# Key weights in three loads, x in four copies, and a new order for all work, in an attention and GLU kernel

## Chip, cores and metric

One NeuronCore of one Trainium2 chip runs the whole kernel. The metric is device time in microseconds (us), lower is better. Shorter names for the engines: PE is TensorE (matmuls; PEld its weight loads), DVE is VectorE, ACT is ScalarE, POOL is GpSimd, SP is SyncE, which here only issues DMAs.

## What is computed

x has 2048 tokens of 512 values in bf16. The output is a gated mix of two branches:

```python
g = sigmoid((x * gate_w).sum(-1))
a = A(x, wq, wk, wv, wo, beta)     # 32 heads of 16, 4 segments of 512 tokens
b = B(x, w_gate, w_up, w_down)     # (gelu(x @ w_gate) * (x @ w_up)) @ w_down, 1792 wide
out = g * a + (1 - g) * b
```

In A, each segment has causal softmax attention within itself (`a_dot`), and reads a memory that earlier segments wrote: `a_mem = phi(q) M / phi(q) z`, where `phi(t)` is `t + 1` above zero and `exp(t)` below, `M` sums `phi(k)` times v, and `z` sums `phi(k)`. The two are mixed by `sigmoid(beta)` of the head, and the result is multiplied by `wo`.

## The kernel before

The work is cut into some thousand tasks: a task is one or several instructions of one engine, with what it reads and writes (L68, class Task). The order of all tasks is a list written into the file, `ORDER`; `schedule` (L129) walks it, takes the PSUM bank that stands behind the colon for a task that opens one (`K0_1a:1`), or the engine for an eviction that may run on two (`Kev0_0:d` is DVE, `:a` is ACT). Each engine then runs its own tasks in the order of the list, and `finalize` (L189) puts a semaphore wait in front of an instruction for what other engines or DMAs must have done first. So a task that waits holds up everything behind it on its engine, and SP's queue of DMA issues is one such engine. The place of a load in the list does not say when it is issued: SP issues each as soon as its own waits and those ahead of it are over.

Names of tasks, with segment s and tile t of four:

- `ld_...`: loads (`ld_w`, L340 to 341). x of segment 0 comes in two ways: tokens 0 to 255 as two plain loads of 128 KB (`ld_x0_0` on SP, `ld_x0_1` on ACT), and tokens 256 to 511 by two transposing DMAs (`ld_x0_t2`, `ld_x0_t3`, L361). The key weights come as two loads of 256 KB, blocks 2 and 3 on SP (`ld_wk1`), blocks 0 and 1 on ACT (`ld_wk0`).
- `warm1`, `warm2` (L383): matmuls on constants that only keep PE busy. `xtr0_p` (L786): PE transposes of the first 256 tokens into PSUM; `xev0_p` (L795): copies of them to SBUF.
- `K0_ta`, `K0_tb`, `K0_tc` (L477): key projections of segment 0, in blocks 2 and 3 on the first 256 tokens, blocks 0 and 1 on them, and all blocks on tokens 256 to 511. `Ks_t`, `Qs_t`, `Gs_ft`, `Us_ft` (L449): other projections, 4 matmuls of 512 columns each. `Vs_ma`, `Vs_mb` (L499): value projections. `Kev`, `Qev`, `Gev`, `Vev` (L442 to 443, L506 to 507): evictions from PSUM.
- `kpada`, `kpadb` (L488): masked copies of the keys that the score matmuls load as weights.
- `sts_tA` to `E` (L602): fills of PSUM with scores; there is one PSUM area for them. `exps_...` (L609): the exponential of a fill on ACT, 2048 wide; the next fill waits for it. `msks_...` (L615): causal masks on POOL. `pvs_t` (L644): reads of the values, 128 small matmuls for two tiles, which take half of the values from `vsh`, a copy with the partitions' halves swapped.
- `vshs_mj` (L518): DMAs on SP that make `vsh`. `ktrs_t` (L573): DMA transposes of phi(k); `otrs_c` (L564): of the memory's output.
- `pha`, `phb`, `phc` (L461 to 465): phi on DVE, ACT, DVE. `mz` (L577), `nd` (L547): memory write and read on PE.
- `gelu`, `gd` (L698, L703): gelu on ACT; `h` (L720): the product with the up projection; `out` (L735), `wo` (L749): last products; `wev`, `oev` (L740 to 753): their evictions; `dma` (L757): stores.
- `ld_beta`, `betab` (L764): the heads' gates, loaded and copied. `ld_gw`, `gwz`, `gwtr`, `gwev` (L354, L769, L771): the gate vector, made into a 513th column of the value weights.

Of the kernel before, what the change touches and what calls it, by code (L numbers as in the profile page):

```python
# [248 lines left out]
def _build(es, nc, A_x, A_wq, A_wk, A_wv, A_wo, A_beta, B_w_gate, B_w_up, B_w_down, gate_w, out):  # L249
# [132 lines left out]
    for name, n, cols in (("warm1", 45, 80), ("warm2", 7, 80)):  # L382
        one(name, PE, 3.0, [I(lambda e, cols=cols: e.matmul(BK[s0.i][:, 0:cols], ones, ones[:, 0:cols], start=True, stop=True),  # L383
                              [], [bk(s0)]) for _ in range(n)], bias=9000.0, opens=name == "warm1")
# [400 lines left out]
    for p in (1, 0):  # L785
        one(f"xtr0_{p}", PE, 4 * T_TR, [I(lambda e, q=q, kb=kb, p=p: e.transpose(  # L786
            XB[:, 1024 * p + (kb % 2) * 256 + q * 128:1024 * p + (kb % 2) * 256 + q * 128 + 128],
            pt[stage[0]][:, q, kb * 128:(kb + 1) * 128], ident[:, :]),
            [("xs", 0, 0), ("xs", 0, 1), ("pt", stage[0]), ("ident",)], [("X", p)]) for kb in (2 * p, 2 * p + 1) for q in (0, 1)])
        dst = xT[0][:, 2 * p:2 * p + 2, 0:256]  # L790
        xin = XB[:, 1024 * p:1024 * p + 512].rearrange("p (k c) -> p k c", c=256)
        wr = [("xT", 0, kb, "h0") for kb in (2 * p, 2 * p + 1)]
        task(f"xev0_{p}", [
            (ACT, 0.477, [I(lambda e, dst=dst, xin=xin: e.activation(dst, xin, ACTF.Copy), [("X", p)], wr)]),
            (DVE, 0.335, [I(lambda e, dst=dst, xin=xin: e.tensor_copy(dst, xin), [("X", p)], wr)])], L_DVE)  # L795
# [67 lines left out]
ld_x0_0 ld_wk1 ld_x0_1 warm1:0 ident xtr0_1 xev0_1:d xtr0_0 warm2 xev0_0:d vones0 masks ld_wk0 causal1 gwz ld_x0_t2 ld_x0_t3 ld_wq0 ld_wq1 ld_gw  # L863
causal0 consts K0_1a:1 K0_3a:2 K0_3b K0_2a:3 K0_0a:0 K0_2b K0_0b K0_1b K0_0c K0_2c K0_3c K0_1c Kev0_0:d Kev0_2:d kpadb0_0 kpadb0_2 causal kpada0_0
Kev0_3:a Q0_0:0 ld_wg0b Qev0_0:a Q0_1:3 st0_0A gwtr:2 Kev0_1:d gwev Q0_3:0 ld_wv ld_wg0 Qev0_1:d V0_1b:1 V0_3a:2 V0_3b:3 exp0_0A Qev0_3:d Vev0_3a:a
Vev0_1b:a st0_0B Vev0_3b:d kpada0_2 kpada0_1 V0_0b:0 V0_1a:2 V0_2a:1 Vev0_0b:d G0_6:3 Gev0_6:d Vev0_1a:d Vev0_2a:d exp0_0B st0_0C exp0_0C Q0_2:0
G0_2:3 V0_2b:2 ld_x1_2 ld_x1_1 ld_x1_3 ld_x1_0 ld_beta st0_0D Vev0_2b:a exp0_0D Gev0_2:d kpadb0_1 Qev0_2:d phka0_0 V1_2b:1 V0_0a:3 G1_6:2 V1_0b:0
Vev1_2b:d phka0_2 st0_0E Vev0_0a:d Vev1_0b:d G0_1:1 Gev1_6:a exp0_0E Gev0_1:d Q1_2:3 V1_3b:2 V1_3a:0 kpada0_3 Qev1_2:d Vev1_3a:d phkb0_2 phkc0_2
Vev1_3b:d st0_1A gz0 exp0_1A gr0 Q1_0:1 V1_0a:3 G1_5:0 Vev1_0a:d Gev1_5:d st0_1B Q1_1:2 K1_0:3 exp0_1B phkb0_0 ld_wu1 ld_x2_0 G0_5:0 Qev1_0:d kpadb0_3
vsh0_21 st0_1C exp0_1C Qev1_1:d ld_x2_1 ld_x2_3 ktr0_3 ld_wg1 Gev0_5:d V1_2a:1 K1_3:2 K1_1:0 vsh0_01 Vev1_2a:a vsh0_20 ld_x2_2 ktr0_2 vsh0_00 ld_wd1  # L870
st0_1D phkc0_0 betab Kev1_1:d kpada1_1 G0_4:1 G0_3:0 Gev0_4:d Kev1_0:d Gev0_3:d Kev1_3:a ld_wd0 ld_wu0 ktr0_1 ktr0_0 vsh1_20 ld_wo V1_1a:2 Vev1_1a:d
exp0_1D bexp st0_2A exp0_2A msk0_0B msk0_0D msk0_0C kpada1_0 msk0_0E goa0 gob0 msk0_0A msk0_1A msk0_1C msk0_1D gqa gfull msk0_1B G0_0:1 Q1_3:3 G1_1:0
Qev1_3:d phqa1_0 st0_2B Gev0_0:d gqb Gev1_1:a pv0_1:2301 exp0_2B tp0_d01 tp0_d00 pvp0_01 Q2_0:3 Qev2_0:d tp0_d11 st0_2C K1_2:2 Kev1_2:d pvp0_00
tp0_d10 gelu0 G0_8:3 G0_13:1 gd0_13 G0_10:2 G0_11:0 G0_9:1 gd0_8 gd0_10 gd0_9 gd0_11 G0_12:3 G0_7:2 gd0_12 G1_2:1 U0_0:0 gd0_7 Gev1_2:d pvp0_11 h0_0
U0_13:3 U0_10:2 h0_10 Q2_1:1 Qev2_1:d exp0_2C st0_2D mz0:0 U0_7:2 U0_9:1 pvp0_10 h0_13 exp0_2D phqb1_0 st0_2E exp0_2E phka1_0 h0_7 mza0 h0_9 ota0_0
phqa1_2 kpadb1_0 G1_4:3 U0_1:2 h0_1 Gev1_4:a V1_1b:0 st0_3A G1_0:1 U0_5:3 Q2_2:2 exp0_3A Vev1_1b:a Gev1_0:a Qev2_2:a kpadb1_1 st0_3B exp0_3B U0_11:0
U0_4:1 U0_12:2 st0_3C phkb1_0 exp0_3C phqc1_0 kpada1_2 h0_4 h0_5 U0_6:1 U0_2:3 h0_11 h0_12 phqb1_2 h0_2 G1_3:0 Gev1_3:d h0_6 kpadb1_2 st0_3D phka1_2
U0_3:2 h0_3 U0_8:3 h0_8 Q2_3:0 Qev2_3:d exp0_3D phkb1_2 msk0_2A msk0_2B msk0_2C msk0_3A msk0_2E msk0_2D msk0_3C goc0 msk0_3B st1_0A msk0_3D pv0_3:1230
exp1_0A st1_0B exp1_0B tp0_d20 tp0_d21 pvp0_20 tp0_d30 ota0_1 pvp0_21 tp0_d31 kpada1_3 out0_1_0:1 out0_1_1 out0_1_2 V2_0a:2 Vev2_0a:d G1_9:3 V2_1b:0
Vev2_1b:d wev0_1:d st1_0C G1_8:2 G1_10:0 G1_11:1 gelu1 gd1_9 G1_7:3 gd1_8 gd1_10 gd1_7 gd1_11 G1_13:2 gd1_13 G1_12:0 gd1_12 phqc1_2 phkc1_0 mzq0  # L880
pvp0_31 pvp0_30 ota0_3 V2_0b:3 Vev2_0b:d ota0_2 V2_1a:1 Vev2_1a:d out0_0_0:2 out0_0_1 out0_0_2 nd1_0:0 ndp1_0 phkc1_2 exp1_0C st1_0D exp1_0D K2_0:3
K2_2:1 wev0_0:d Kev2_0:d Kev2_2:a K2_1:0 st1_0E Kev2_1:d U1_2:2 h1_2 wo0_1:1 nd1_3:3 nd1_1:0 exp1_0E st1_1A ld_x3_2 vsh1_00 vsh2_01 ktr1_1 ktr1_0
oev0_1 ndp1_1 wo0_0:2 oev0_0 kpada2_0 vsh1_21 out0_2_0:1 nd1_2:0 msk1_0C msk1_0A exp1_1A st1_1B exp1_1B msk1_0B gz1 msk1_0E msk1_1A msk1_0D msk1_1B
out0_2_1 wo0_2:2 ndp1_2 st1_1C exp1_1C nd1_5:0 out0_2_2 ndp1_3 wev0_2:a ndp1_5 out0_3_0:3 st1_1D nd1_4:0 out0_3_1 out0_3_2 ktr1_2 dma0 vsh1_01 otr1_3
ndp1_4 otr1_0 oev0_2 phka2_0 msk1_1C wev0_3:d ktr1_3 dma1 vsh2_00 otr1_1 ld_x3_1 ld_x3_0 ld_x3_3 exp1_1D st1_2A exp1_2A gr1 msk1_1D pv1_1:1023 st1_2B
exp1_2B tp1_d01 tp1_d00 kpadb1_3 V2_2b:0 Vev2_2b:d K2_3:1 Kev2_3:a G2_3:0 pvp1_00 Gev2_3:d tp1_d10 st1_2C U1_8:1 G2_1:0 otr1_2 V2_3a:2 h1_8 Gev2_1:d
Vev2_3a:d kpadb2_0 kpadb2_1 exp1_2C st1_2D phkb2_0 exp1_2D G2_6:1 wo0_3:0 U1_3:2 pvp1_01 tp1_d11 Gev2_6:a h1_3 phka2_2 oev0_3 st1_2E U1_0:3 V2_3b:1
G2_0:2 Gev2_0:d h1_0 Vev2_3b:d exp1_2E phkb2_2 st1_3A mz1:0 G2_4:2 G2_5:3 pvp1_10 mza1 Gev2_5:d exp1_3A st1_3B exp1_3B Gev2_4:d U1_11:1 G2_2:0
Gev2_2:d ota1_0 U1_13:3 h1_13 U1_10:2 h1_10 h1_11 G2_11:0 G2_10:3 pvp1_11 phkc2_0 phkc2_2 ota1_1 otm1_0 otm1_1 G2_12:2 G2_9:1 st1_3C gelu2 gd2_11
gd2_12 G2_7:0 G2_13:2 gd2_10 gd2_9 gd2_7 gd2_13 G2_8:3 gd2_8 U1_7:1 U2_9:0 K3_0:2 h1_7 U2_5:3 Q3_0:1 phqa2_0 h2_9 h2_5 Qev3_0:d Kev3_0:d exp1_3C  # L890
st1_3D exp1_3D U1_1:0 U2_12:3 msk1_3A msk1_2A msk1_3B U2_13:1 h2_12 h1_1 h2_13 kpada2_1 st2_0A U1_9:2 V2_2a:3 U2_7:0 msk1_2D msk1_2B msk1_2E h1_9
Vev2_2a:d vsh2_20 dma2 dma3 ktr2_0 ktr2_2 vsh2_21 exp2_0A phqb2_0 msk1_3D msk1_2C msk1_3C st2_0B h2_7 kpada2_2 pv1_3:1230 tp1_d21 exp2_0B tp1_d20
V3_1a:2 Vev3_1a:a st2_0C exp2_0C pvp1_21 tp1_d31 U1_6:1 Q3_1:2 V3_0a:0 st2_0D h1_6 pvp1_20 Vev3_0a:d Qev3_1:a V3_2b:1 U1_4:2 U1_5:0 exp2_0D st2_0E
exp2_0E tp1_d30 phqc2_0 h1_5 h1_4 ota1_2 Vev3_2b:a U1_12:3 h1_12 pvp1_31 pvp1_30 out1_1_0:0 st2_1A V3_1b:2 out1_1_1 V3_3a:3 exp2_1A st2_1B msk2_0B
msk2_0D Vev3_3a:a exp2_1B out1_1_2 U2_4:1 msk2_0E goa1 gob1 kpadb2_3 kpada2_3 msk2_0C msk2_0A msk2_1A ota1_3 h2_4 otm1_2 otm1_3 K3_1:3 mzq1 Vev3_1b:a
wev1_1:a st2_1C msk2_1B goc1 U2_1:2 Q3_3:1 V3_0b:0 Kev3_1:d kpada3_0 h2_1 Qev3_3:d kpadb2_2 exp2_1C msk2_1C st2_1D V3_2a:3 U2_6:2 exp2_1D Vev3_2a:a
wo1_1:1 Vev3_0b:d kpadb3_0 h2_6 oev1_1 st2_2A msk2_1D pv2_1:0231 exp2_2A st2_2B exp2_2B tp2_d00 pvp2_00 phqa2_2 tp2_d01 tp2_d10 pvp2_10 pvp2_01
tp2_d11 out1_0_0:0 out1_0_1 st2_2C phqb2_2 out1_0_2 V3_3b:2 Vev3_3b:d wev1_0:d out1_3_0:3 phqc2_2 pvp2_11 exp2_2C st2_2D exp2_2D wo1_0:1 out1_3_1
# [46 lines left out]
```

## Time and profile before

| | us |
|---|---|
| median of 3 runs | 263.83 (263.21 to 263.96) |
| the profiled execution | 264.41 |
| its span, first to last instruction | 262.7 |
| PE busy in it | 254.5 |
| ACT busy | 203.2 |
| DVE busy | 198.1 |

The profile is of one execution. Its rows give start and duration in us from the span's start, line, engine, operation, tiles written and read, and in brackets the idle time of the engine before and what ended it. A row of a group gives busy time, the mean duration in ns, and the idle time just ahead of the group's instructions.

### The profile page before, as it was taken

What the parts mean: (1) busy time and instruction counts of PE and PEld (TensorE: products, weight loads), DVE (VectorE), ACT (ScalarE), POOL (GpSimd) and SP (SyncE); (2) the same over time, 40 slices, a digit from 0 to 9 for tenths busy, and PEclk for the clock granted to TensorE, in tenths of its full rate; (3) what the DMA queues carried; (4) which work ended last, traced back from release to release, by engine and by line L of the source; (5) the groups of instructions that cost most, each with busy time, mean ns of one, the idle gap of its engine ahead of it and who ended that gap; (6) DMA issues with size and microseconds to landing.
All of it is one profiled execution on the core that took longest, in us unless ns stands there. A gap on an engine that the chain in (4) does not pass through costs nothing.

```text
span 262.7 us, 6672 instructions
## 1 busy us (share of the span) xinstructions
PE 254.5 (97%) x2815; PEld 122.6 (47%) x2849; DVE 198.1 (75%) x412; ACT 203.2 (77%) x171; POOL 98.3 (37%) x163
## 2 busy tenths in 40 slices
PE   7999999999999999999999999999999999999995
...
DMA packets 31990, 16.50 MB, mean 63 GB/s; under 512 B 21592, under 2 KB 31960, under 8 KB 31960
## 3 DMA queue, kind: packets, MB, share of 16 engines
...
q10 hardware_dynamic: 688, 0.85, 0.9%
...
## 4 chain that ended last, share of the span: by engine, by line
PE 88%; DVE 6%; ACT 3%; issue 2%; DVEq 0%
PE psD L449 41%; PE psD L735 19%; PE psX L602 8%; PE psD L644 6%; PE psD L749 5%; PE psD L499 5%; PE psD L547 1%; ACT gb L698 1%; PE psD L383 1%; PE psD L477 1%; DVE kT L443 1%; DVE gb L443 1%; ACT pt L609 1%; PE psD L577 1%; DVE phk L461 1%
## 5 line engine op out<-in xcount | busy, mean ns | idle before, releaser
L609 ACT ACTIVATE pt<-psX 128x2048 bf16<-128x2048 f32 x72 | 135.1, 1877 | 28.3 <-PE psX L602 26.7
L615 POOL TENSOR_TENSOR pt<-pt,ctri 128x256 bf16<-128x256 bf16 x128 | 91.7, 727 | 129.4 <-ACT pt L609 124.9
L449 PE MATMUL psD<-xT,wu 128*128 128x512 bf16 x214 | 52.7, 380 | 1.3 <-issue 1.1
L449 PE MATMUL psD<-xT,wg 128*128 128x512 bf16 x216 | 52.3, 379 | 0.8 <-issue 0.3
L735 PE MATMUL psD<-wd,gb 128*128 128x512 bf16 x217 | 51.8, 379 | 0.8 <-issue 0.5
L720 DVE TENSOR_TENSOR gb<-psD,gb 128x512 bf16<-128x512 f32 x56 | 37.2, 681 | 10.8 <-PE psD L449 10.8
L449 PEld LDWEIGHTS psD<-xT,wg 128*128 128x128 bf16 x224 | 20.7, 98 | 24.7 <-issue 1.3
L735 PEld LDWEIGHTS psD<-wd,gb 128*128 128x128 bf16 x224 | 20.7, 98 | 24.3 <-issue 2.1
L449 PEld LDWEIGHTS psD<-xT,wu 128*128 128x128 bf16 x224 | 20.2, 98 | 24.8 <-issue 2.6
L602 PE MATMUL psX<-qT,kD 32*128 32x192 bf16 (+7 forms) x512 | 28.5, 287 | 0.0
L530 DVE STREAM_TRANSPOSE tT<-psD 128x512 f32<-128x512 f32 x32 | 21.7, 701 | 5.5 <-PE psD L644 5.0
L443 DVE CAST gb<-psD 128x512 bf16<-128x512 f32 x20 | 13.6, 687 | 12.8 <-PE psD L449 12.8
L602 PEld LDWEIGHTS psX<-qT,kD 32*128 32x128 bf16 x512 | 8.2, 92 | 25.1 <-ACT pt L609 13.6
L499 PE MATMUL psD<-wv,xT 128*128 128x257 bf16 (+1 forms) x128 | 18.2, 273 | 0.0
L753 DVE SCALAR_TENSOR_TENSOR ost<-psD,gtok,wds 128x512 bf16<-128x512 f32 (+1 forms) x17 | 11.9, 710 | 7.9 <-PE psD L749 7.8
L668 DVE SCALAR_TENSOR_TENSOR ob<-tT,gq,rc 128x256 bf16<-128x256 f32 x32 | 16.7, 522 | 1.1
L703 ACT ACTIVATE gb<-psD 128x512 bf16<-128x512 f32 x28 | 15.0, 595 | 3.3 <-PE psD L449 3.3
L644 PE MATMUL psD<-pt,vsh 64*17 64x192 bf16 (+7 forms) x512 | 17.1, 283 | 0.0
L644 PE MATMUL psD<-pt,vnat 64*17 64x192 bf16 (+7 forms) x512 | 17.1, 283 | 0.0
L449 PE MATMUL psD<-xT,wq 128*128 128x512 bf16 x60 | 15.6, 379 | 0.4 <-issue 0.2
L749 PE MATMUL psD<-wo,oT 128*128 128x512 bf16 (+1 forms) x66 | 15.7, 367 | 0.2 <-issue 0.2
L499 PEld LDWEIGHTS psD<-wv,xT 128*128 128x128 bf16 x128 | 11.8, 97 | 6.6 <-issue 1.3
...
## 6 DMA issues: line engine op xcount, KB each, us to landing
...
vsh<-vnat SPq DMA_DIRECT2D x16, 68.0 KB, 2.7
...
wq<-in_A_wq_dram SPq DMA_DIRECT2D x2, 256.0 KB, 3.7
...
```

The costliest lines, as they stand in the source:

```text
L443: (DVE, 0.60, [I(lambda e: e.tensor_copy(dst, src()), [bk(sl), *reads], writes)]),
L449: one(name, PE, n * T_MM, [I(lambda e, i=i: e.matmul(BK[sl.i][:, :], lhs(i), rhs(i), start=(i == 0), stop=(i == n - 1)), reads(i), [bk(sl) ...
L499: one(f"V{s}_{m}{'ab'[hf]}", PE, 2 * T_MM, [I(lambda e, i=i, sl=sl, a=a, z=z, xs=xs: e.matmul(BK[sl.i][:, 0:z - a], xs(i), wv[:, i, a:z], ...
L530: one(f"tp{name}", DVE, 0.605, [I(lambda e, sl=sl, ti=ti: e.transpose(tT[ti][:, :], BK[sl.i][:, :]), [bk(sl)], [("tT", ti)])], bias=bias)
L602: ins.append(I(lambda e, t=t, kb=kb, ncol=ncol, c0=c0, g=g: e.matmul(XALL[:, g * 512 + c0:g * 512 + c0 + ncol], kD[(4 * s + t) % R_KD][32 ...
L609: one(f"exp{s}_{name}", ACT, 2048 * 0.000833 + 0.05, [I(lambda e: e.activation(pt[slot][:, :, :], xin, ACTF.Exp, scale=ATT_SCALE), [("X",) ...
L615: ins.append(I(lambda e, mv=mv: e.tensor_tensor(mv, mv, cm, ALU.mult), [("pt", slot), ("causal",)], [("pt", slot)]))
L644: ins.append(I(lambda e, kb=kb, slot=slot, c0=c0, n=n, g=g, r0=r0, sl=banks[j], va=va: e.matmul(BK[sl.i][32 * g:32 * g + 17, 64 * kb:512], ...
L668: I(lambda e, ti=ti, ri=ri, t=t, j=j, dst=dst: e.scalar_tensor_tensor(out=dst, in0=t_rows(ti), scalar=gq[:, 2 * t + j:2 * t + j + 1], in1= ...
L720: one(f"h{s}_{ft}", DVE, 0.605, [I(lambda e, sl=sl, gi=gi, f=f: e.tensor_tensor(gb[gi][:, f, :], BK[sl.i][:, :], gb[gi][:, f, :], ALU.mult ...
L735: mm.append(I(lambda e, fb=fb, gi=gi, f=f, q=q, sl=sl: e.matmul(BK[sl.i][:, :], gb[gi][:, f, q], wd[:, fb, :], start=(fb == 0), stop=(fb = ...
L749: one(f"wo{s}_{qt}{sfx}", PE, 4 * T_MM * w / 512, [I(lambda e, kb=kb, q=q, so=so, c=c, w=w: e.matmul(BK[so.i][:, 0:w], oT[:, kb, q], wo[:, ...
```

## The change

The loads of the key weights are three, in the queues of SP, ACT and ACT; the transposes and copies of x go by block, four of each on smaller tiles; the warming matmuls are one run of 52 with 66 columns:

```diff
-    for eng, h in ((SP, 1), (ACT, 0)):
-        ld_w(f"wk{h}", eng, wk[:, halves[h], :], wsrc(A_wk)[:, halves[h], :], [("wk", 2 * h), ("wk", 2 * h + 1)], 0.25)
+    for eng, nm, c in ((SP, "2", slice(2, 3)), (ACT, "3", slice(3, 4)), (ACT, "0", slice(0, 2))):
+        ld_w(f"wk{nm}", eng, wk[:, c, :], wsrc(A_wk)[:, c, :], [("wk", i) for i in range(c.start, c.stop)], 0.125)
...
-    for name, n, cols in (("warm1", 45, 80), ("warm2", 7, 80)):
+    one("warm1", PE, 3.0, [I(lambda e: e.matmul(BK[s0.i][:, 0:66], ones, ones[:, 0:66], start=True, stop=True),
+                             [], [bk(s0)]) for _ in range(52)], bias=9000.0, opens=True)
...
-    for p in (1, 0):
-        one(f"xtr0_{p}", PE, 4 * T_TR, [...
+    for kb in (2, 3, 0, 1):
+        one(f"xtr0_{kb}", PE, 2 * T_TR, [...
...
-            (DVE, 0.335, [I(lambda e, dst=dst, xin=xin: e.tensor_copy(dst, xin), [("X", p)], wr)])], L_DVE)
+            (DVE, 0.25, [I(lambda e, dst=dst, xin=xin: e.tensor_copy(dst, xin), [("X", kb)], wr)])], L_DVE)
```

The list `ORDER` is another one throughout. Its beginning before:

```
ld_x0_0 ld_wk1 ld_x0_1 warm1:0 ident xtr0_1 xev0_1:d xtr0_0 warm2 xev0_0:d vones0 masks ld_wk0 causal1 gwz ld_x0_t2 ld_x0_t3 ld_wq0 ld_wq1 ld_gw
causal0 consts K0_1a:1 K0_3a:2 K0_3b K0_2a:3 K0_0a:0 K0_2b K0_0b K0_1b K0_0c K0_2c K0_3c K0_1c Kev0_0:d Kev0_2:d kpadb0_0 kpadb0_2 causal kpada0_0
Kev0_3:a Q0_0:0 ...
```

and after:

```
ld_x0_1 ld_wk3 ld_wk0 warm1:0 ld_x0_0 causal1 ident xtr0_2 xtr0_3 xtr0_0 xtr0_1 vones0 ld_wk2 ld_x0_t2 ld_x0_t3 ld_wq0 gwz xev0_3:d masks xev0_1:a
xev0_0:a xev0_2:d K0_1a:1 K0_3a:2 K0_0a:3 K0_3b K0_1b K0_2a:0 K0_1c Kev0_1:d K0_3c Kev0_3:a kpadb0_1 kpadb0_3 K0_0b K0_0c K0_2b Kev0_0:a phka0_0
kpada0_0 ld_wq1 ld_gw ld_wg0b ld_wv ld_wg0 Q0_0:1 Q0_2:2 ... st0_0A exp0_0A K0_2c ...
... Gev0_2:d Qev0_2:d G0_5:1 V1_2b:3 G1_6:2 betab kpada0_1 Gev1_6:d st0_0E ...
... exp0_1C K1_3:2 Vev1_2a:a phkc0_2 st0_1D Kev1_1:d kpada1_1 G0_3:0 G0_4:1 vsh1_20 vsh0_20 vsh0_00 ld_wd1 ktr0_2 exp0_1D Gev0_4:a kpadb0_2 st0_2A exp0_2A ... Q1_3:3 V1_1a:0 Vev1_1a:a G0_0:1 st0_2B ... pv0_1:3021 ...
```

SP's queue from the second segment's x on was, before: `vsh0_21`, x of segment 2, `ktr0_3`, `ld_wg1`, `vsh0_01`, `vsh0_20`, x, `ktr0_2`, `vsh0_00`, `ld_wd1`, `ld_wd0`, `ld_wu0`, `ktr0_1`, `ktr0_0`, `vsh1_20`, `ld_wo`. After, it is: `ktr0_0`, `vsh0_21`, x, `vsh0_01`, `ld_wg1`, x, `vsh1_20`, `vsh0_20`, `vsh0_00`, `ld_wd1`, `ktr0_2`, `ktr0_3`, `ld_wd0`, `ld_wu0`, `ktr0_1`, and so on, with `ld_wo` behind the second segment's transposes.

More of the change, by code (lines that the diff above doesn't have):

```diff
@@ L381, in _build @@
     ones = nc.const_aps.tensor(1.0, [P, P], BF)
-    for name, n, cols in (("warm1", 45, 80), ("warm2", 7, 80)):
-        one(name, PE, 3.0, [I(lambda e, cols=cols: e.matmul(BK[s0.i][:, 0:cols], ones, ones[:, 0:cols], start=True, stop=True),
-                              [], [bk(s0)]) for _ in range(n)], bias=9000.0, opens=name == "warm1")
+    one("warm1", PE, 3.0, [I(lambda e: e.matmul(BK[s0.i][:, 0:66], ones, ones[:, 0:66], start=True, stop=True),
+                             [], [bk(s0)]) for _ in range(52)], bias=9000.0, opens=True)
     cn = [
@@ L784, in _build @@
     XB = XALL.bitcast(BF)
-    for p in (1, 0):
-        one(f"xtr0_{p}", PE, 4 * T_TR, [I(lambda e, q=q, kb=kb, p=p: e.transpose(
-            XB[:, 1024 * p + (kb % 2) * 256 + q * 128:1024 * p + (kb % 2) * 256 + q * 128 + 128],
+    for kb in (2, 3, 0, 1):
+        one(f"xtr0_{kb}", PE, 2 * T_TR, [I(lambda e, q=q, kb=kb: e.transpose(
+            XB[:, 1024 * kb + q * 128:1024 * kb + q * 128 + 128],
             pt[stage[0]][:, q, kb * 128:(kb + 1) * 128], ident[:, :]),
[L789 to L795, printed above, removed]
+            [("xs", 0, 0), ("xs", 0, 1), ("pt", stage[0]), ("ident",)], [("X", kb)]) for q in (0, 1)])
+        dst, xin, wr = xT[0][:, kb, 0:256], XB[:, 1024 * kb:1024 * kb + 256], [("xT", 0, kb, "h0")]
+        task(f"xev0_{kb}", [
+            (ACT, 0.38, [I(lambda e, dst=dst, xin=xin: e.activation(dst, xin, ACTF.Copy), [("X", kb)], wr)]),
+            (DVE, 0.25, [I(lambda e, dst=dst, xin=xin: e.tensor_copy(dst, xin), [("X", kb)], wr)])], L_DVE)
     head_gates()
@@ L862 @@
 ORDER = """
[L863 to L898, printed above, removed]
@@ L899 @@
-st2_2E nd2_0:2 out1_2_0:0 out1_3_2 msk2_2C gz2 gr2 gz3 gr3 goa3 ndp2_0 gob3 oev1_0 msk2_2D goc3 goa2 gob2 exp2_2E st2_3A exp2_3A msk2_3A msk2_2B
-wev1_3:d G3_4:2 nd2_2:1 out1_2_1 Gev3_4:a ndp2_2 st2_3B exp2_3B nd2_4:3 G3_1:1 Gev3_1:d out1_2_2 nd2_1:2 st2_3C dma4 ktr2_1 vsh3_20 vsh3_01 ktr2_3
-dma5 ndp2_4 ndp2_1 G3_3:1 wo1_3:3 exp2_3C Gev3_3:a K3_2:2 st2_3D wev1_2:a msk2_2A kpada3_1 oev1_3 Kev3_2:d nd2_5:1 nd2_3:3 G3_0:0 G3_5:2 ndp2_3 ndp2_5
-Gev3_0:d msk2_3C msk2_2E exp2_3D st3_0A exp3_0A goc2 msk2_3D msk2_3B G3_2:3 wo1_2:1 Gev3_2:d G3_6:0 Gev3_6:a Gev3_5:d oev1_2 ota2_0 st3_0B pv2_3:3210
```

14 lines of the change are left out of this document (1 added, 13 removed).

## The prediction

> **What bounds the kernel now.** I read the page's shares and slices first, then who waited for whom on PE, then the chain that ended last, then the first 12 us in order of time.
>
> ```profile
> span 262.7 us, 6672 instructions
> PE 254.5 (97%) x2815; PEld 122.6 (47%) x2849; DVE 198.1 (75%) x412; ACT 203.2 (77%) x171; POOL 98.3 (37%) x163
> ...
> PE   7999999999999999999999999999999999999995
> ...
> PE 88%; DVE 6%; ACT 3%; issue 2%; DVEq 0%
> ...
> L449 PE MATMUL psD<-xT,wu 128*128 128x512 bf16 x214 | 52.7, 380 | 1.3 <-issue 1.1
> ```
>
> The second row gives PE 254.5 of 262.7 us; the slices show it full from the second to the last but one. A busy PE need not be a fast one, since matmuls overlap, so I look for idle time and for the pace:
>
> ```profile
> PE psD L477 <- DVE omem L354: 0.6, 1, 0.6
> PE psD L449 <- issue: 1.8, 11, 0.2
> ```
>
> ```profile
> 0.82 3.16 PE psD L383 x45
> ...
> 5.30 0.38 issue
> 5.91 2.71 PE psD L477 x20
> ...
> 9.97 1.67 PE psD L449 x7
> ...
> 12.97 1.32 PE psD L499 x12
> ...
> 16.90 0.33 PE psX L602 x8
> 17.23 1.85 PE psD L449 x8
> ...
> 42.86 8.31 PE psD L449 x38
> ...
> 258.00 0.82 PE psD L749 x3
> 258.91 0.60 issue
> ```
>
> The only wait of PE above 0.2 us is the 0.6 before the first key projection (L477; the release is put down to a memset, but the chain shows plain waiting from 5.30). After it, 38 matmuls of 512 columns take 8.31 us, 0.216 each, at the end of the span as in the middle. So **PE is the bound from 5.9 us to the tail**. The change adds no PE work behind the head: the same projections, fills, reads and outputs stand in both orders. A new order can therefore gain only in the head, or lose by making PE wait. The forecast is a sum of differences on the profiled 264.41 us; that run is 0.58 above the median of 263.83 (263.21 to 263.96), and I put the same difference on the median.
>
> **The head.** Rows in order of time, and the landing times of the DMAs:
>
> ```profile
> 1.22 0.46 ACTq L341 DMA_DIRECT2D wk<-in_A_wk_dram  x1
> 1.25 0.41 SPq L341 DMA_DIRECT2D wk<-in_A_wk_dram  x1
> ...
> 3.78 1.05 PE L786 MATMUL psX<-ident,pt 128*128 128x128 bf16 x8
> ...
> 4.44 0.85 DVE L795 COPY xT<-psX 128x512 bf16<-128x512 bf16 x2 [4.44 <-PE psX L786]
> ...
> 5.91 4.01 PE L477 MATMUL psD<-xT,wk 128*128 128x256 bf16 x32 [0.61 <-DVE omem L354]
> ...
> 6.77 0.39 SPq L341 DMA_DIRECT2D wv<-in_A_wv_dram  x1
> ```
>
> ```profile
> wk<-in_A_wk_dram ACTq DMA_DIRECT2D x1, 256.0 KB, 5.0
> wk<-in_A_wk_dram SPq DMA_DIRECT2D x1, 256.0 KB, 4.5
> ```
>
> ```profile
> L361 SPq DMA_TRANSPOSE xT<-in_A_x_dram x2: 1261/1272/1282, 1.7 to 3.0; - x2
> ...
> DMA to landing us min/median/max: 4.2/4.6/5.0
> ```
>
> SP's half of the key weights (blocks 2 and 3, the ones used first) lands at 1.25 + 4.5 = 5.75, and the first projection starts at 5.91. x is copied by 4.44 + 0.85 = 5.29, so the weights were last, by about 0.5 us.
>
> In the changed kernel blocks 2 and 3 come as 128 KB each, SP and ACT, second in their queues; blocks 0 and 1 are ACT's third. Half the bytes stand before the first projection. x is copied in four parts, xev0_3 and xev0_2 on DVE, 1 and 0 on ACT. The transposes to PSUM are the same eight. xev0_3 can start at 4.44 as before; two copies of half the size cost at least the 0.42 of one big one and, with a fixed share, about 0.58, so the first projection can start at 5.0 to 5.1: **at most 0.83 sooner** (5.91 - 5.08). The split gives x itself nothing.
>
> How much of that lives? The third group of key matmuls (columns 256 on) needs both DMA transposes of x; the second is issued at 1.71 + 1.28 + the queue, 3.04, and lands 4.2 later, at 7.24 (the other at 1.7 + 5.0 = 6.7, which is when wv, waiting for it, is issued: 6.77). Before, 16 small matmuls stand in front of that group; in the new order 12 do (K0_1a 3a 0a, K0_3b 1b, K0_2a). Twelve at 0.11 (12 in 1.32) are 1.3 us, a little more while the pace is slow, so from 5.1 they end at about 6.6 to 7.0, and K0_1c waits until 7.3. From there 20 of 32 are left: the last would start at 7.3 + 19 x 0.11 = 9.39, against 9.92 - 0.27 = 9.65 before. **Head: -0.26.** Bounds: -0.83 (all of it kept) and +0.45 (the pieces land like ACT's half, 1.22 + 5.0 = 6.22, and twelve matmuls follow). The query weights follow SP's transposes in both; gate vector: gwz is moved ahead of the copies on DVE, so its load no longer waits for that memset, but wv behind it still waits for the 6.7 landing. Worth nothing, and its use, gwtr, stands far behind. The 52 warming matmuls of 66 columns in one run instead of 45 and 7 of 80 end before x lands: nothing, unless the pace changes (rival 3).
>
> **A later limit on the lead.** In the new order DVE runs betab ahead of kpada0_1, which the fill st0_0E needs; before, betab came at 32 us.
>
> ```profile
> 16.08 0.58 SPq L341 DMA_DIRECT2D omem<-in_A_beta_dram  x1
> ```
>
> ```profile
> omem<-in_A_beta_dram SPq DMA_DIRECT2D x1, 8.0 KB, 4.9
> ```
>
> ```profile
> 19.71 0.34 DVE L488 TENSOR_SCALAR kD<-kT,maskB 128x512 bf16<-128x512 bf16 x1
> ...
> 22.05 0.40 PE L602 MATMUL psX<-qT,kD 32*128 32x256 bf16 x8
> ...
> 32.56 1.25 DVE L764 COPY betab<-omem 32x8 bf16<-32x8 bf16 x4
> ```
>
> Beta lands at 16.08 + 4.9 = 20.98 in either order, since SP's queue before it is paced by wv. With 1.25 for the four copies (0.7 if nothing slows the last) and 0.34 for kpada, st0_0E's second half can go at 22.0 to 22.6. The row at 22.05 is st0_0E before; in the new order G0_5 (0.86 by the pace) stands ahead of it in place of V1_0b (0.44), so with the lead of 0.26 PE is there at 22.2, and at the second half 0.15 later. I take 0.1, bounds 0 to 0.3. Any further lead would be lost here.
>
> **One fill too early.** A fill, its exponential and the next fill form a loop:
>
> ```profile
> 213.50 0.40 PE L602 MATMUL psX<-qT,kD 32*128 32x448 bf16 x8
> ...
> 213.96 1.88 ACT L609 ACTIVATE pt<-psX 128x2048 bf16<-128x2048 f32 x1 [0.42 <-PE psX L602]
> ...
> 215.89 0.40 PE L602 MATMUL psX<-qT,kD 32*128 32x384 bf16 x8
> ```
>
> That is 2.39 from fill to fill. Wherever the PE work between two fills is shorter, PE waits. The old order has at least eight big and three small matmuls between any two. The new one has st0_1D, G0_3, G0_4, st0_2A: 0.33 + 1.85 = 2.18 (the rows at 16.90 and 17.23). **+0.2**, and nothing else can fill it, since PE is in order. Bounds 0 to 0.3.
>
> **The rest.** I compared, fill by fill, the PE work with ACT's work between exponentials. From st0_2B the two orders have nearly the same intervals; at two places ACT has an eviction or a phi exponential more than before (st2_0A, st2_1D). Each overruns by under 0.1. I take +0.1, bounds -0.3 (small waits that the old order has and the new has not) to +0.5. The tail has the same last five groups on PE and the same evictions: 0.
>
> Sum: -0.26 + 0.1 + 0.2 + 0.1 = +0.14, so **264.0 us**. This case's own range is 263.2 to 264.7.
>
> **Rivals.**
>
> 1. *The lead is kept.* SP's queue holds 128 KB less ahead of the transposes; if they land half a microsecond sooner, 0.83 can stay: 263.83 - 0.83 = 263.0. For it: wk alone was late. Against it: the same bytes move in all, and beta. 262.6 to 263.4.
>
> 2. *The shifted V copies become the wait (slower).* In SP's queue vsh1_20 now stands ahead of vsh0_20 and vsh0_00, which the first value read pv0_1 needs. vsh1_20 waits for Vev1_2a, an ACT eviction right behind exp0_1C (0.38). Two issues of 0.61 follow, so vsh0_00 is issued 1.6 us after exp0_1C ends. PE reaches pv0_1 after st0_1D to st0_2A (2.39), st0_2A to st0_2B (0.33 + 2.26), and st0_2B (0.33): 5.4 us after it. That leaves 3.8 for the landing.
>
> ```profile
> 32.93 0.38 ACT L507 ACTIVATE vnat<-psD 128x256 bf16<-128x256 f32 x1
> ```
>
> ```profile
> vsh<-vnat SPq DMA_DIRECT2D x3, 68.0 KB, 4.6
> ```
>
> ```profile
> L518 SPq DMA_DIRECT2D vsh<-vnat x16: 597/611/1514, 24.5 to 194.0; - x16
> ...
> DMA to landing us min/median/max: 2.0/2.7/6.1
> ```
>
> The first of these is from 30 to 35.2 us, behind a 896 KB load, as here. It decides at 3.8: at 4.6 PE loses 0.8 (264.8), at 6.1 2.3 (266.3). For it: the loads of this stage. Against it: one transpose fewer in front, and 2.7 over all. I give it 264.9.
>
> 3. *The slow pace lasts longer.* 45 matmuls of 80 columns take 3.16 us, 0.070 each, while 256 columns later take 0.11: PE starts at half pace although the granted clock shows full in every slice. The key matmuls still begin slow: 31 x 0.11 and one of 0.27 are 3.7, they take 4.01, so some three ran at half pace. The new head has 728 columns less of warming (52 x 66 against 52 x 80), none of it between the transposes and the first projection. [...] From rows: with all 32 key matmuls at half pace they take 32 x 0.11 = 3.5 more, less the 0.3 paid already. I take half of that, 264.0 + 1.6 = 265.6, between 264.4 and 267.2.
>
> 4. *The pieces are not reported sooner.* ACT's half, issued first, landed 0.5 us after SP's. If wk3 on ACT waits for the transposes, K0_1a stands at 6.2: the +0.45 above instead of -0.26, 264.7 at most, 264.5 with what the slow pace no longer costs. [...]
>
> **How the numbers follow.** Forecast 0.37, rival 1 0.20, rival 2 0.21, rival 3 0.12, rival 4 0.10. About 0.3% (0.8 us) is what a measurement of this kernel can tell from no change: under 263.04 is faster, over 264.62 slower. Faster: 0.14 of rival 1 and 0.03 of the forecast, 0.17. Slower: 0.18 of rival 2, 0.12 of rival 3, 0.03 of rival 4, 0.04 of the forecast, 0.37. Within: 0.46. The range, with a tenth left out at each end: 262.9 to 265.7.
>
> **What would show it.** The first L477 matmul at 5.0 to 5.2 and a gap of PE before the matmuls of the third group; a wait of a fill for DVE (kD) near 22 us; a wait of L602 for ACT near 35 us of 0.2; no PE gap at the first L644. Wrong if L477 starts at 5.9 or later, if its 32 matmuls take over 5 us without a gap (rival 3), if L644 waits for a DMA (rival 2), or if PE idles somewhere after 60 us, where I saw no cause.

## The result, and the profile after

The changed kernel took **266.03 us** (median of 6 runs, 264.96 to 266.90), the kernel before 263.75 (6 runs, 263.00 to 263.96): ratio 1.0084, 95% interval 1.0065 to 1.0104. The forecast was 264.0, with a range up to 265.7. (The same kernel in another set of six runs, a_again below, has a median of 265.31.) The runs of the changed kernel lie twice as far apart as those before. Its profiled execution took 265.86, span 264.1: 1.45 us over the profiled 264.41.

From the page of the changed kernel (its lines from 383 on stand one lower than before, L643 for L644):

```profile
span 264.1 us, 6703 instructions
...
PE   8999999999999999999999999999999999899995
...
q8 instruction: 22, 0.36, 0.6%
...
PE 89%; DMA 5%; SPq 2%; issue 1%; DVE 1%; ACT 1%; DVEq 0%
```

TensorE is as full as before, but for a dent near the end, and a DMA has come into the chain. Who waited for whom on TensorE in the changed kernel:

```profile
PE psD L643 <- issue: 0.9, 1, 0.9
PE psD L382 <- PEq L875: 0.8, 1, 0.8
PE psX L601 <- DVE kD L487: 0.4, 1, 0.4
PE psD L476 <- DVE xT L792: 0.4, 1, 0.4
PE psX L601 <- ACT pt L608: 0.2, 1, 0.2
```

L382 is the warming, L476 the first keys. Three lines are new: a fill (L601) waits 0.4 for VectorE's kD, a fill waits 0.2 for ScalarE, and a value matmul (L643) stands 0.9 us for "issue", which means for nothing that the profile shows. The places, in order of time on TensorE:

```profile
4.96 3.79 PE L476 MATMUL psD<-xT,wk 128*128 128x256 bf16 x28 [0.36 <-DVE xT L792]
```

```profile
22.44 0.29 PE L601 MATMUL psX<-qT,kD 32*128 32x256 bf16 x4 [0.41 <-DVE kD L487]
```

```profile
226.03 0.31 PE L643 MATMUL psD<-pt,vnat 64*17 64x320 bf16 x4
227.25 0.26 PE L643 MATMUL psD<-pt,vsh 64*17 64x192 bf16 x4 [0.91 <-issue]
```

The first is the head: keys begin at 4.96, 0.95 before the old 5.91. The second is the second half of st0_0E behind beta. The third stands in the middle of pv3_1, the 128 value matmuls at 224 us: 112 are done, and the next ones start 1.2 us later.

To compare the two orders I use TensorE's **lag**: the start of a group less the work of all matmuls from the first key on (from the first key to the last group of four 251.9 us in both orders). "Behind pv3_1" is the next fill, st3_2C. b_before and a_again are second profiles of the kernel before and of the changed kernel; a_store6 and a_beta are edits of the latter, shown further down.

```
                first key   st0_0E  st0_1A  st0_2A  pv3_1  behind pv3_1   last
before            5.88       6.28    6.29    6.41    7.00      6.99       7.11
b_before          5.66       5.83    5.84    5.96    6.52      6.51       6.63
after             4.96       5.54    6.14    6.47    7.17      8.48       8.59
a_again           4.85       5.64    6.55    6.88    7.59      7.79       7.90
a_store6          4.73       5.25    6.11    6.44    7.17      8.79       8.91
a_beta            4.73       5.17    5.18    5.50    6.20      6.39       6.51
```

After less before, in the two profiles first shown: head -0.74, beta's fill +0.59 (0.60 against 0.01), st0_1A to st0_2A +0.21, from there to pv3_1 +0.11, pv3_1 +1.32, the rest -0.01. Sum +1.48, against 1.45 of the clock. The table says more. The pause in pv3_1 is in some executions only; a_again, without it, has +0.20 in that column, so that 1.1 of the 1.32 is the pause. Beta costs 0.60 to 0.91, and the old head of b_before is 0.45 better than that of the first profile.

### The profile page after: what moved, and what is told of

It is laid out like the page before. It is cut to its first block, busy times and chain, and to the rows that moved or that the text cites. A ratio compares the mean times of both kernels' runs of the same rounds, so it can differ in the third digit from the quotient of the medians.

```text
span 264.1 us, 6703 instructions
## 1 busy us (share of the span) xinstructions
PE 258.1 (98%) x2849; PEld 121.8 (46%) x2849; DVE 195.7 (74%) x403; ACT 207.5 (79%) x182; POOL 96.9 (37%) x163
## 4 chain that ended last, share of the span: by engine, by line
PE 89%; DMA 5%; SPq 2%; issue 1%; DVE 1%; ACT 1%; DVEq 0%
PE psD L448 44%; PE psD L734 19%; PE psX L601 9%; PE psD L643 6%; PE psD L748 5%; PE psD L498 4%; SPq L345 2%; DMA omem<-in_A_beta_dram 2%; DMA xT<-in_A_x_dram 2%; DMA wv<-in_A_wv_dram 2%; PE psD L546 1%; ACT pt L608 1%; PE psD L576 1%; DVE ost L752 0%; SPq L341 0%
## 5 line engine op out<-in xcount | busy, mean ns | idle before, releaser
L614 POOL TENSOR_TENSOR pt<-pt,ctri 128x256 bf16<-128x256 bf16 x128 | 89.2, 708 | 128.1 <-ACT pt L608 105.2
L448 PE MATMUL psD<-xT,wu 128*128 128x512 bf16 x224 | 54.7, 380 | 0.0
L719 DVE TENSOR_TENSOR gb<-psD,gb 128x512 bf16<-128x512 f32 x56 | 37.9, 685 | 21.5 <-PE psD L448 21.0
L734 PE MATMUL psD<-wd,gb 128*128 128x512 bf16 x224 | 53.5, 380 | 0.0
L448 PE MATMUL psD<-xT,wg 128*128 128x512 bf16 x224 | 53.0, 379 | 0.0
L601 PE MATMUL psX<-qT,kD 32*128 32x192 bf16 (+7 forms) x512 | 28.7, 287 | 0.7 <-DVE kD L487 0.4
L601 PEld LDWEIGHTS psX<-qT,kD 32*128 32x128 bf16 x512 | 8.4, 92 | 26.0 <-ACT pt L608 10.9
L643 PE MATMUL psD<-pt,vsh 64*17 64x192 bf16 (+7 forms) x512 | 17.4, 283 | 0.9 <-issue 0.9
L702 ACT ACTIVATE gb<-psD 128x512 bf16<-128x512 f32 x28 | 15.6, 593 | 3.1 <-PE psD L448 2.8
L498 PE MATMUL psD<-wv,xT 128*128 128x256 bf16 (+1 forms) x128 | 17.9, 273 | 0.0
L643 PE MATMUL psD<-pt,vnat 64*17 64x192 bf16 (+7 forms) x512 | 17.4, 283 | 0.0
L739 ACT ACTIVATE wds<-psD,omgt 128x512 f32<-128x512 f32 x7 | 4.7, 685 | 12.6 <-PE psD L734 12.6
```

What stands on the lines that cost most here:

```text
L448: one(name, PE, n * T_MM, [I(lambda e, i=i: e.matmul(BK[sl.i][:, :], lhs(i), rhs(i), start=(i == 0), stop=(i == n - 1)), reads(i), [bk(sl) ...
L498: one(f"V{s}_{m}{'ab'[hf]}", PE, 2 * T_MM, [I(lambda e, i=i, sl=sl, a=a, z=z, xs=xs: e.matmul(BK[sl.i][:, 0:z - a], xs(i), wv[:, i, a:z], ...
L601: ins.append(I(lambda e, t=t, kb=kb, ncol=ncol, c0=c0, g=g: e.matmul(XALL[:, g * 512 + c0:g * 512 + c0 + ncol], kD[(4 * s + t) % R_KD][32 ...
L614: ins.append(I(lambda e, mv=mv: e.tensor_tensor(mv, mv, cm, ALU.mult), [("pt", slot), ("causal",)], [("pt", slot)]))
L643: ins.append(I(lambda e, kb=kb, slot=slot, c0=c0, n=n, g=g, r0=r0, sl=banks[j], va=va: e.matmul(BK[sl.i][32 * g:32 * g + 17, 64 * kb:512], ...
L702: t = one(f"gd{s}_{ft}", ACT, 0.485, [I(lambda e, gi=gi, f=f, sl=sl: e.activation(gb[gi][:, f, :], BK[sl.i][:, :], ACTF.Gelu_apprx_tanh), ...
```

## The experiments

The runs a_, b_, c_, d_ and e_ are five sets, each on a chip of its own, beside runs of the kernel before on the same chip; that one's medians lay between 263.56 and 263.64.

### a_again, a_split4, a_store6, a_beta: which of the losses counts

a_again is the changed kernel unedited.

> The changed kernel once more, nothing edited. In its first profile TensorE stood still for 1.2 us (226.04 to 227.25) in the middle of the 128 value matmuls pv3_1, waiting for nothing that the profile names, and a 16 KB packet of the instruction queue q8 had begun at 224.54 and taken 1.32 us. Theory F (the instruction block that holds the rest of pv3_1 comes too late): the pause is at the same matmul again, 0.5 to 2 us long, and the time is 265 to 267. Theory B (the loss sits in the head, where st0_0E waits for beta, and the pause was an accident of one execution): no pause in pv3_1, the time is still 265.5 to 266.5, and the wait before the second half of st0_0E is 1 us or more.

265.31 (264.23 to 265.72, 6 runs), ratio 1.0064 (1.0042 to 1.0086). Its profile has no pause in pv3_1, and a longer wait for beta; each theory has a part right: the time is in F's range, and the pause is missing as B said, but the wait before the second half of st0_0E is 0.7 where B said 1 or more. TensorE's waits in a_again:

```profile
PE psX L601 <- DVE kD L487: 0.7, 1, 0.7
PE psD L476 <- DMA wk<-in_A_wk_dram: 0.3, 1, 0.3
```

a_split4:

```
+ cuts = (slice(0, 256), slice(256, 512)) if name in ("U2_10", "U2_2", "U3_13", "U2_11") else (slice(0, 512),)
- one(name, ..., [I(lambda e, i=i: e.matmul(BK[sl.i][:, :], lhs(i), rhs(i), ...)) for i in range(n)], ...)
+ one(name, ..., [I(lambda e, i=i, c=c: e.matmul(BK[sl.i][:, c], lhs(i), rhs(i)[:, c], ...)) for c in cuts for i in range(n)], ...)
```

> The changed kernel with four of its up projections between pv2_3 and pv3_1 (U2_10, U2_2, U3_13, U2_11) written as two half-wide matmuls for each full one: the same work, but 32 more TensorE instructions ahead of pv3_1, so that every border between instruction blocks lies 32 instructions earlier in the program from there on. Theory F: the fetch is then asked for well before pv3_1, the pause in pv3_1 is gone, and the time is 264.3 to 264.9 (266.0 less the 1.3 that the pause cost, or a little more). Theory B: the borders do not matter, the time is 266.0 or up to 0.1 more. Should the fetch be asked for no earlier, the pause only moves 16 matmuls ahead within pv3_1.

264.70 (264.21 to 266.46, 11 runs): the median as by theory F and no pause in its profile, but five runs at 265.4 to 266.5. With beta still in the way these runs prove neither.

a_store6:

```
- oev1_2 msk2_2D ... st3_2E dma6 msk3_2C
+ oev1_2 dma6 msk2_2D ... st3_2E msk3_2C
```

> The changed kernel with the store of output tile 6 issued directly behind oev1_2 (near 187 us) in place of 223.99, so that one store and not two (223.60 and 223.99) is under way when the instruction block for pv3_1 is fetched at 224.54. Theory S (the two stores hold the fetch up on the DMA engines): the packet takes 0.9 to 1.0 us in place of 1.32, the pause is shorter by 0.4 us or gone, the time is 264.5 to 265.6. Theory F without S (the fetch is asked for too late, whatever the stores do): the pause stays over 0.8 us and the time is 265.6 to 266.2.

265.83 (264.30 to 266.67, 6 runs). The pause is there, longer than in the first profile, so the second store alone is not its cause. TensorE in a_store6:

```profile
227.56 0.26 PE L643 MATMUL psD<-pt,vsh 64*17 64x192 bf16 x4 [1.23 <-issue]
```

a_beta:

```
- betab kpada0_1 Gev1_6:d st0_0E
+ kpada0_1 Gev1_6:d betab st0_0E
```

> The changed kernel with VectorE's copy of beta moved behind kpada0_1 and Gev1_6, so that the second half of st0_0E no longer waits for beta's load (issued 16.26, landed 21.23). Theory F: the 0.4 us wait before st0_0E goes, of which 0.2 to 0.5 is kept to the end, and the pause in pv3_1 stays: 265.5 to 265.8. Theory B: most of the loss goes, 264.0 to 264.8.

265.76 (263.78 to 266.47, 8 runs). The profiled run is the fastest; in it both losses are absent, and st0_0E goes through in one piece, 1.1 us before the second half of the changed kernel:

```profile
21.36 0.40 PE L601 MATMUL psX<-qT,kD 32*128 32x256 bf16 x8
```

The lag stays at 5.17 over st0_0E: beta's wait is gone. Yet six of the eight runs lie over 265.

### b_split12, b_fix, b_newhead, b_before: one at a time

b_split12 has the same edit for U2_3, U2_8, U2_0, U2_10, U2_2, U2_11, U3_13, U3_1, U3_7, G3_7, G3_13, G3_12, 96 more TensorE instructions ahead of pv3_1; b_fix has that and a_beta's.

> The changed kernel with twelve up and gate projections between pv2_3 and pv3_1 written as two half-wide matmuls for each full one: 96 more TensorE instructions there, so that the border between instruction blocks that fell 37 instructions ahead of pv3_1 falls 133 ahead of it. Theory F (the refill of instructions for pv3_1 is asked for at 221 to 222 in some executions and only at 224.6 in others, and then pv3_1 stands still for 1.2 to 1.5 us): no execution has the pause, so the upper half of the runs goes, the median is 264.4 to 264.9 and the highest run under 265.5. Theory V (the scatter has another source, in the head or the loads): the runs still reach from 264.2 to over 266, as with 32 more instructions.

264.77 (264.24 to 265.97, 9 runs), no pause in the profile, 0.8 of wait for beta. The median came as theory F said, the highest run did not.

> The same twelve projections in halves, and beta's copy behind kpada0_1 and Gev1_6 as well. If the two losses add: no wait before the second half of st0_0E, no pause in pv3_1, TensorE reaches pv0_1 at 37.5 to 37.9 (39.34 in the kernel before), and the median is 263.6 to 264.0 with no run over 264.8. If beta's wait is paid later anyway, by the fills: 264.3 to 264.8.

264.51 (264.34 to 264.92, 5 runs). **In these five runs the scatter is gone**: a_beta, 96 instructions away from it, reached from 263.78 to 266.47 in eight. But the median is 0.9 over the kernel before, not level with it: the two losses are not all.

b_newhead takes the changed kernel's order up to xev0_2, and from there the old order of all that is left:

```
  ld_x0_1 ld_wk3 ld_wk0 warm1:0 ... xev0_1:a xev0_0:a xev0_2:d
- K0_1a:1 K0_3a:2 K0_0a:3 K0_3b K0_1b ...
+ ld_wq1 ld_gw causal0 consts K0_1a:1 K0_3a:2 K0_3b K0_2a:3 K0_0a:0 ...
```

> The new head alone (three key pieces, four parts of x, one warming run) with the old order of all work behind it. Theory H (the new head is worth what TensorE's earlier start shows, and the old order keeps it): first key matmul near 4.9, 0.4 to 0.8 us under the kernel before, 262.9 to 263.3. Theory P (ScalarE's chain of fills sets the pace until 36 us, and the earlier start runs into it): pv0_1 not earlier than 39.0, and 263.5 to 263.9.

263.85 (263.54 to 265.20, 11 runs) against 263.62, ratio 1.0013 (1.0000 to 1.0025): no gain of the new head alone is seen. One of its runs is at 265.20, though its order behind the head is the old one. In its profile the keys start at 4.85, and the third group waits for the piece that lands last:

```profile
6.00 3.22 PE L476 MATMUL psD<-xT,wk 128*128 128x256 bf16 x28 [0.54 <-DMA wk<-in_A_wk_dram]
```

> The kernel before, unedited, for a second profile. Its first profile took 264.41, 0.58 over the median of the runs shown with it. If that execution's head was late (the loads of x and the keys landing late by chance), the second profile has its first key matmul before 5.9, reaches pv0_1 by about 38.8 and ends with the median near 263.7; TensorE's time from pv0_1 to the end is the same to 0.05 us. If the 0.58 lies elsewhere, the head is the same and a stretch behind pv0_1 is shorter. The instruction block for pv3_1 is fetched at 222 again.

263.92 in its one run: first key 5.66, pv0_1 at 38.89 instead of 39.34, from there to the last matmul 219.93 against 219.96. The first profile of the kernel before had a late head; behind pv0_1 nothing differs.

### c_border, c_mask, c_newhead2

c_border is a_beta's edit with 27 projections in halves (the twelve, G3_0 to G3_3, G3_5, G3_6, G3_8 to G3_11, Q3_2, U3_3, U3_6, U3_8, U3_9).

> The changed kernel with beta's copy behind kpada0_1 and Gev1_6, and with 27 projections between pv2_1 and pv3_1 written as two half-wide matmuls each: 216 more TensorE instructions, so that a border between instruction blocks now lies 3 instructions behind the last semaphore wait ahead of pv3_1 (it was 36 ahead of that wait in the changed kernel, 132 ahead with twelve projections in halves). [...] Theory F: the pause is there in every execution, at the end of pv3_1 or in the first matmuls behind it, 0.7 to 1.5 us long; the median is 265.5 to 266.3 and no run is under 265.0. Theory R (the refill is late at random, and the place of the border has no part in it): some runs are free of it, near 264.7, some over 266, as in the changed kernel.

264.51 (264.00 to 266.02, 11 runs). One run of eleven over 265: theory F's form of it fell. The refill went out at 224.16, behind the wait's end at 223.18, and landed at 225.65; the instruction 256 behind the place of the other pauses came at 227.10, behind pv3_1, and no pause is seen.

c_mask is b_fix with:

```
- exp3_2A msk3_2A msk3_1D wev2_3:a
+ exp3_2A msk3_1D msk3_2A wev2_3:a
```

> Beta's copy moved and twelve projections in halves (264.51 so far), and GpSimd's mask msk3_1D put ahead of msk3_2A. In every profile of the changed order TensorE waits 0.25 us within pv3_1 (0.39 in place of 0.14 us ahead of the matmuls of the last pieces) while GpSimd, without a break from 220 us on, ends its seventh mask at 225.96 to 226.37. If the order of the masks is the cause, the wait goes and the median is 264.2 to 264.4; if it is the number of masks, or if the gain is given back at the next fill, 264.5.

264.24 (263.83 to 264.88, 8 runs), ratio 1.0029 (1.0014 to 1.0043). The wait of 0.25 within pv3_1 is gone, as forecast. In the changed kernel GpSimd makes seven masks in a row, of which msk3_1D is the last that pv3_1 needs, and TensorE's weight loads stand for it:

```profile
220.11 5.85 POOL L614 TENSOR_TENSOR pt<-pt,ctri 128x256 bf16<-128x256 bf16 x7
...
226.01 0.09 PEld L643 LDWEIGHTS psD<-pt,vsh 64*17 64x17 bf16 x4 [0.31 <-POOL pt L614]
```

c_newhead2 is b_newhead with:

```
- K0_1a:1 K0_3a:2 K0_3b K0_2a:3 K0_0a:0 K0_2b K0_0b K0_1b
+ K0_1a:1 K0_3a:2 K0_2a:3 K0_0a:0 K0_3b K0_2b K0_0b K0_1b
```

> The new head with the old order of all work, and in it the first four key groups in the order that the new pieces allow: all four that need only wk2 and wk3 first, then those that need wk0. With the old order of these groups TensorE started the keys at 4.85 and stood still for 0.54 us at the third group until wk0 landed. Theory H: the wait shrinks to 0.1 to 0.3 us, and the gain is kept: 263.2 to 263.6, at or under the kernel before. Theory D (what ends last in the head are x0_t3 and the query weights, so the later groups wait in its place): 263.7 to 263.9.

263.48 (262.95 to 263.99, 11 runs) against 263.60, ratio 0.9995 (0.9983 to 1.0006): level with the kernel before; no other edit has a lower median. The keys run through, 32 from 4.91:

```profile
4.91 3.75 PE L476 MATMUL psD<-xT,wk 128*128 128x256 bf16 x32 [0.16 <-DVE xT L792]
```

### d_border29, d_plain, e_nostore: what makes the refill late

d_border29 has G3_4 and K3_3 in halves too.

> As with 27 projections in halves, and two more (G3_4, K3_3): 16 more TensorE instructions ahead of pv3_1, so that the border lies 4 instructions ahead of the two semaphore waits before pv3_1, and the next border 14 instructions ahead of the end of pv3_1. Theory W (the request for the refill is held while TensorE's queue stands at a semaphore wait, and goes out when the wait is over): the packet starts 0.9 to 1.1 us behind the second wait's end in every execution, pv3_1 stands still for 0.4 to 1.0 us at its last matmuls, and the median is 264.9 to 265.5. Theory R (late at random, whatever stands behind the border): most runs as with 27 halves, 264.5, with one or two near 266. If the request goes out as the border is passed: the packet starts near 222, no pause, 264.5.

265.39 (264.32 to 265.45, 6 runs), inside theory W's range and against W: in the profile (265.41) the refill starts at 222.74, while the waits end at 223.88 and 224.29, and pv3_1 has no pause. That profile lost time at pv0_1, which waits for a V copy:

```profile
PE psD L644 <- DMA vsh<-vnat: 0.8, 1, 0.8
```

d_plain has a_beta's and c_mask's moves and no halves.

> The changed kernel with two moves and nothing written in halves: beta's copy behind kpada0_1 and Gev1_6, and the mask msk3_1D ahead of msk3_2A. The border is back where the changed kernel has it, 36 instructions ahead of the last semaphore wait before pv3_1. Theory F (late refills come with this place of the border): a quarter to three quarters of the runs have the pause and lie at 265.2 to 266.4, the others at 263.6 to 264.4; the highest run is over 265.4. If the late refills had another cause, the runs keep within 263.6 to 264.8, like those with twelve halves and both moves (263.83 to 264.88).

265.19 (12 runs): six at 263.87 to 264.86, six at 265.53 to 266.29. **Without the halves the upper group is back**, as theory F said. c_mask, which differs by the halves alone, has none of eight runs over 265; but it ran on another chip. d_border29, on the chip of d_plain, has no run over 265.45. No run of d_plain's upper group was profiled, so that the pause is what lifts these runs is inferred.

e_nostore is d_plain with:

```
- ost = [sb(f"ost{i}", [P, 512]) for i in range(2)]
+ ost = [sb(f"ost{i}", [P, 512]) for i in range(3)]
- wi, oi = gt % R_WD, gt % 2
+ wi, oi = gt % R_WD, 2 if gt == 9 else gt % 2
- oev1_2 msk2_2D ... dma9 st3_2C ... dma6 msk3_2C ... dma8 otr3_3
+ oev1_2 dma6 msk2_2D ... st3_2C ... msk3_2C ... dma8 dma9 otr3_3
```

> The changed kernel with beta's copy and the mask moved, nothing in halves, and with both stores that it issues near 223.6 taken away from there: tile 6 stored directly behind oev1_2 (near 187), tile 9 held back behind tile 8's store (near 236), from a third output buffer of its own. TensorE's program is that of the kernel with the two moves alone, word for word in its order and waits. Theory S (the late refill is tied to the stores: in both late cases seen its packet started 0.1 to 0.2 us behind the first packet of a store): no late refill, all runs 263.8 to 264.9. Theory without S: the two groups of runs stay, at about 264.3 and 265.9, half of the runs in each.

265.21 (264.09 to 266.26, 7 runs): the high runs stay, though here two lie between the groups, at 265.03 and 265.21. The profiled run, 264.56, has a late refill and a pause with no store near, so the stores are not what makes the refill late. The traffic of all DMA engines from 220 to 228 us, 0.2 us a digit, first a_again, then e_nostore:

```profile
GB/s 0 0 0 0 0 0 0 0 0 0 82 0 0 0 0 0 0 0 0 0 0 0 0 0 195 348 169 333 261 5 0 0 0 0 0 0 82 0 0 0
```

```profile
GB/s 0 0 0 0 0 0 0 0 0 0 0 0 0 0 0 0 0 0 82 0 0 0 0 0 0 0 0 0 0 0 0 0 0 0 0 82 0 0 0 0
```

An 82 is one 16 KB packet of queue q8 (16.4 KB in 0.2 us), put down to the slice in which it starts. In a_again the refill stands at 222.0 and the stores behind it; in e_nostore it stands at 223.6, with no store anywhere, and TensorE pauses:

```profile
225.94 0.26 PE L643 MATMUL psD<-pt,vsh 64*17 64x192 bf16 x4 [0.40 <-issue]
```

The refill for pv3_1 in the profiles of the changed kernel and of its edits without halves (the packets of q8 in the traces; the pause is the distance between the two weight loads around it):

```
              packet starts   takes   last wait ahead of pv3_1 ends   pause
a_again          222.08       1.20            224.03                    -
a_beta           221.18       0.88            222.64                    -
d_plain          221.54       1.20            223.40                    -
after            224.54       1.32            223.61                   1.21
a_store6         224.66       1.63            223.61                   1.53
e_nostore        223.65       0.92            223.03                   0.72
```

Three early, three late, and each late one pauses ahead of the same instruction, the 114th of the 128 weight loads of pv3_1. TensorE goes on 1.27 to 1.39 us behind the end of the late packet in all three. So the pause goes with the late refill in all six; that it comes from it is inferred, and what makes it late stays open. All three late packets start 0.6 to 1.1 us behind the last wait's end, as if the request had been held; d_border29, for which the border was reckoned 4 instructions ahead of the waits, was not held. One difference was not tested: in the 9 us ahead of pv3_1 TensorE's queue has wait instructions of its own at 220.71, 223.21 and 223.61 in the changed kernel, and only at 223.62 and 223.75 in the kernel before.

The time of a run alone does not tell of the pause. a_again (265.19), b_split12 (265.62) and d_border29 (265.41) were profiled without one, and e_nostore (264.56) with one.

## Why the prediction was wrong, step by step

**The rest, +0.1, "saw no cause after 60 us": this step failed.** From st0_2A to behind pv3_1 the first profile lost 1.43 in its place, a_again 0.33. The step looked at what each engine does between two fills and missed two things. One is the pause. In the first profile of the changed kernel the instruction queue moves 22 packets of 16,384 bytes, and TensorE has 5,743 recorded instructions; from the start of the first packet (13.50) to that of the last (248.87) 5,365 of them start, 255 to a packet. pv3_1 is 128 matmuls, 256 instructions with their weight loads; 128 such matmuls take 2.08 us where nothing stops them. The pause stands 226 instructions into pv3_1. If that is just behind a border between packets, the border before it lies some 30 instructions or a little more ahead of pv3_1, and a new order of the work ahead moves it: this is an estimate from the 255, since no trace shows a border. The places that the expectations give it (37 ahead of pv3_1, 36 ahead of the last wait, 3 behind that wait, 4 ahead of the two waits) are the author's reckoning and not measured; in the trace of the changed kernel the last three wait instructions stand 51, 20 and 17 instructions ahead of pv3_1. In the six profiles of the table TensorE pauses there where the refill starts at 223.65 to 224.66, and does not where it starts at 221.18 to 222.08; no profile shows such a pause anywhere else. TensorE stands for 0.72 to 1.53 a time, of which 0.6 to 1.4 reach the end. It is in three of the six profiles of the table, and six of twelve runs of d_plain lie in the upper group, 1.6 over the lower, which is a little more than any pause seen. In the kernel before pv3_1 starts only 5 instructions earlier (4,827 of TensorE's ahead of it in the trace, counting a matmul to each weight load, in place of 4,832), its refill starts at 222.03 and 221.14 in two profiles, and of its 91 runs beside the five sets one was over 265; why it is spared is not shown. In the first profile of the changed kernel the pause (0.91 of it put down to "issue") is the only wait of that kind that the matmuls show, with 22 packets in all. The other is the mask msk3_1D behind msk3_2A: 0.2 to 0.25 in every profile that has this order of masks.

**Beta, +0.1 (0 to 0.3): right place, wrong size.** 0.60 to 0.97 in the five profiles that have it. In the first the second half of st0_0E went at 22.44, inside the 22.0 to 22.6 of the sum; the wait was longer because TensorE came sooner. "Any further lead would be lost here" held: against the first profile of before, head and beta together gave -0.15 (6.14 against 6.29), and the sum had -0.16. But the end of that wait is set by beta's landing and not by TensorE: its copies start at 21.26 as the load lands, 0.73 after VectorE is free, and at 21.7 in a_again. With that the lag behind it is 6.14 in the first profile, 6.55 in a_again and 6.79 in b_split12: here the path took on the load's scatter.

**The head, -0.26.** Against the first profile -0.74 at st0_0E, against b_before -0.29. The pieces landed early (wk2 at 4.08, wk3 at 4.29), so rival 4 fell. TensorE's weight loads for the keys in the changed kernel:

```profile
4.96 0.55 PEld L476 LDWEIGHTS psD<-xT,wk 128*128 128x128 bf16 x6 [0.53 <-DVE xT L792]
...
5.88 0.56 PEld L476 LDWEIGHTS psD<-xT,wk 128*128 128x128 bf16 x6 [0.38 <-issue]
...
6.81 1.66 PEld L476 LDWEIGHTS psD<-xT,wk 128*128 128x128 bf16 x16 [0.36 <-issue]
```

The stop at the third group is there, as the sum had it, but it ends at 6.84 and not at 7.3: the second transpose landed at 6.70, not 7.24. With that the sum gives 6.84 + 19 x 0.11 = 8.93 against 9.65, -0.72, so this landing is the mis-sized term. In b_before it landed at 6.80 too, so most of it is scatter. (Rival 1's condition, transposes half a microsecond sooner, was thus met in that profile; beta took most of the gain.) The stop at the seventh matmul, until 5.91 behind wk0 (landed 5.78), the sum did not have. In between, the key matmuls start 0.11 apart from the first on, so rival 3 fell; in the first profile the first four start 0.17 to 0.21 apart, in b_before the first two.

Alone the new head gave no gain (1.0013): in b_newhead wk0 landed at 5.86, and the keys stood 0.54 for it. With all groups that need only wk2 and wk3 put first, which is not the order of the change, c_newhead2 has 0.9995; the two intervals overlap a little.

**The base.** "I put the same difference on the median" failed: of the 0.58 by which the first profile lay above its median, 0.45 was a late head (keys 0.22 later than in b_before, the rest its slow first matmuls), so a head gained against that profile is not gained against the median.

**The early fill, +0.2,** was right: +0.21, a wait of 0.2 for ScalarE at 35.6.

**Rival 2** did not decide in the first profile: pv0_1 started at 38.56, the copies had landed at 38.02 and 38.25. (The times that the rival adds up to 5.4 come to 5.3.) Its mechanism was real: of the seven profiles with beta's copy moved, three have a wait of pv0_1 for the copies, 0.3 (d_plain), 0.4 (c_mask), 0.8 (d_border29). That, the early fill and 0.1 to 0.15 for the halves (from pv0_1 to the last matmul 221.23 and 221.24 us in place of 221.09 and 221.12) are what the traces have for the 0.64 that c_mask still lies over the kernel before.
